# Attention and MoE kernel on one core: Q of six batches loaded four tokens to a partition, and the query order within 64 tokens carried through to the rows of the output stores

## Chip, cores and metric

One core of a Trainium2 chip. The metric is the device time of the kernel in microseconds (us). One run of before took 1761.32 us; it is not used.

## The reference, cut to what matters

```python
# q, k, v: [8, 8, 576, 64] f32; moe_w_in [512, 2048]; moe_w_out [2048, 512]
scores = q @ k.T / sqrt(64); causal, window of 64 keys; softmax; @ v
x = attn.transpose(0, 2, 1, 3).reshape(4608, 512)
h = x @ w_in
out = (h * clip(h + 3, 0, 6) / 6) @ w_out        # [4608, 512] f32
```

## The kernel before

Attention of a batch (576 tokens) runs between the matmuls of the MoE, which works in nine stages T = 0..8 of 512 tokens. A batch b >= 2 is prepared by DMA: load Q, K, V; cast on GpSimd to bf16; two DMA transposes give QT and KT (head dimension on partitions). Its result `opg` goes by three DMA transposes and one on TensorE into `xT`, from which the next MoE stages read. All these DMAs and the output stores are issued by SyncE, in one order.

```python
def load_blocks(t, src, b, kbs, tail=0):          # 128 tokens to 128 partitions: runs of 256 B
    ...
        out.append(nc.sync.dma_start(
            out=t[p0 : p0 + ss, kb, :, :],
            in_=src[b, :, s0 : s0 + ss, :].rearrange("h s d -> s h d"),
        ))

def load_for_dma(b):
    sts, ins = [], []
    for n, src in (("qst", q), ("kst", k), ("vst", v)):
        t = stage.tile([P, KB, H, D], F32, name=n, tag=n)
        ins += load_blocks(t, src, b, range(KB), SR if src is v else 0)
        sts.append(t)
    return tuple(sts), ins

# scores of a pair of heads, then exp on ScalarE and a multiplication by the mask on VectorE
nc.tensor.matmul(st[:, h, o0 : o0 + n], lhsT=bt.KT[...k0 : k0 + P], rhs=bt.QT[...q0 : q0 + n], ...)

# second MoE matmul: 128 tokens to PSUM partitions, copied by ScalarE and stored
nc.scalar.copy(out=osb[:], in_=accs[ts])
...
nc.sync.dma_start(out=out[u0 : u0 + P, :], in_=osb[:])     # 256 KB, rows in order

for T in range(1, NTB):                            # order of issue
    p1, p2 = pieces(nxt); b = T + 2
    if b < B:
        sts, _ = load_for_dma(b)                   # loads of batch T + 2
        ...                                        # casts in the first half of stage T,
        ...                                        # QT, KT transposes late in its second half
    stage_(T, None, p1, p2)                        # attention of batch T + 1, and stores of stage T
```

The softmax here doesn't subtract the row's maximum and nothing guards it: scores larger than these inputs give would overflow.

Of the kernel before, what the change touches and what calls it, by code (L numbers as in the profile page):

```python
# [9 lines left out]
F32 = mybir.dt.float32  # L10
BF16 = mybir.dt.bfloat16
EXP = mybir.ActivationFunctionType.Exp
RELU = mybir.ActivationFunctionType.Relu
MULT = mybir.AluOpType.mult
# [10 lines left out]
def kernel(  # L25
# [9 lines left out]
    nc = tc.nc  # L35
    P = nc.NUM_PARTITIONS
    B, H, S, D = q.shape
# [4 lines left out]
    KB = (S + P - 1) // P  # L42
    SP = KB * P
    R = 4
    SM = P * R
    SR = S - SM
# [4 lines left out]
    QW = P + WINDOW  # L51
# [3 lines left out]
    consts = ctx.enter_context(tc.tile_pool(name="consts", bufs=1))  # L55
    stage = ctx.enter_context(tc.tile_pool(name="stage", bufs=1))
# [31 lines left out]
    def load_blocks(t, src, b, kbs, tail=0):  # L88
        out = []
        for kb in kbs:  # L90
            s0 = kb * P
            ss = min(P, S - s0)
            p0 = tail if ss < P else 0
# [4 lines that stand above are left out]
        return out  # L98

    def load_qk_for_pe(b, heads):  # L100
        qst = stage.tile([P, H, R * D], F32, name="qst", tag="qst")
        kst = stage.tile([P, H, R * D], F32, name="kst", tag="kst")
        rst = stage.tile([P, H, D], F32, name="rst", tag="rst")
        ins = []
        for h0 in range(0, H, heads):
            for dst, src in ((qst, q), (kst, k)):
                ins.append(nc.sync.dma_start(
                    out=dst[:, h0 : h0 + heads, :],
                    in_=src[b, h0 : h0 + heads, 0:SM, :].rearrange("h (p j) d -> p h (j d)", j=R),
                ))  # L110
            if h0 == 0:
                for i, src in enumerate((q, k)):
                    ins.append(nc.sync.dma_start(
                        out=rst[i * SR : (i + 1) * SR, :, :],
                        in_=src[b, :, SM:S, :].rearrange("h s d -> s h d"),
                    ))
        return (qst, kst, rst), ins
# [5 lines left out]

    def load_for_dma(b):
        sts, ins = [], []
        for n, src in (("qst", q), ("kst", k), ("vst", v)):
            t = stage.tile([P, KB, H, D], F32, name=n, tag=n)
            ins += load_blocks(t, src, b, range(KB), SR if src is v else 0)
            sts.append(t)
        return tuple(sts), ins  # L130

    ctx.enter_context(tc.manual_schedule())
    def load_first():
# [28 lines left out]
    def keep_busy(n):  # L162
# [11 lines left out]
        out=mask1[:], in_=mask1[:], pattern=[[1, QW]], compare_op=ISGE,  # L174
# [3 lines left out]
        out=mask1[:], in_=mask1[:], pattern=[[-1, QW]], compare_op=ISGE,  # L178
        fill=0.0, base=WINDOW - 1, channel_multiplier=1,
    )  # L180
    qn_all = consts.tile([P, NG, KB, 2, D], BF16, name="qn")
    kn_all = consts.tile([P, NG, KB, 2, D], BF16, name="kn")
# [3 lines left out]
    for o0, m0, m1 in ((0, 0, QW), (QW, 0, QW), (2 * QW, 0, QW), (3 * QW, 0, P), (3 * QW + P, WINDOW, P)):  # L186
        nc.vector.tensor_scalar(
            out=maskneg[:, o0 : o0 + m1 - m0], in0=mask1[:, m0:m1],
# [25 lines left out]
    fill_v(0)  # L214

    mask = consts.tile([P, 2 * (KB - 1), QW], BF16, name="mask")

    win16 = consts.tile([P, NG, FF], BF16, name="win16")
    wout16 = consts.tile([P, NFC, DM], BF16, name="wout16")
# [14 lines left out]
    vcopy, pcopy, acopy = nc.vector.tensor_copy, nc.gpsimd.tensor_copy, nc.scalar.copy  # L234

    class Batch:
# [10 lines left out]
            copy(out=self.V[SR:P, KB - 1, :, 0:D], in_=vst[SR:P, KB - 1, :, :])  # L247

        def cast_for_dma(self, st, which=(0, 1, 2)):
            for n, s in [((qn_all, st[0]), (kn_all, st[1]))[i] for i in which if i < 2]:  # L250
                for g in range(NG):
                    pcopy(  # L252
                        out=n[:, g, 0 : KB - 1, :, :].rearrange("p k h d -> p k (h d)"),
                        in_=s[:, 0 : KB - 1, 2 * g : 2 * g + 2, :].rearrange("p k h d -> p k (h d)"),
                    )
                pcopy(
                    out=n[:SR, :, KB - 1, :, :].rearrange("p g h d -> p g (h d)"),
                    in_=s[:SR, KB - 1, :, :].rearrange("p (g h) d -> p g (h d)", h=2),
                )
            if 2 in which:  # L260
                self.cast_v(st[2], 0, H, pcopy)
                self.cast_v_end(st[2], pcopy)
# [66 lines left out]
    def scores(bt, g, u, bias=False, bank=None):  # L329


        pT = P_ring[(bt.b * NG + g) % NPT]
        st = ps_st.tile([P, 2, 512], F32, name=f"st{u if bank is None else bank}")
        w = 2 * QW
        if bias:
            for h in range(2):
                nc.tensor.matmul(
                    st[:, h, 0:w], lhsT=ident[:], rhs=maskneg[:, u * w : (u + 1) * w],
                    start=True, stop=False,
                )  # L340
        blocks = (
            ((0, 0, 0, QW), (QW, P, P, QW)),
            ((0, 2 * P, 2 * P, QW), (QW, 3 * P, 3 * P, P), (QW + P, S - P, SM, SR)),
        )[u]
        for o0, k0, q0, n in blocks:
            for h in range(2):
                nc.tensor.matmul(  # L347
                    st[:, h, o0 : o0 + n],
                    lhsT=bt.KT[h * D : (h + 1) * D, g, k0 : k0 + P],
                    rhs=bt.QT[h * D : (h + 1) * D, g, q0 : q0 + n],  # L350
                    start=not bias, stop=not bias or o0 == blocks[-1][0],
                )

        def exps():
            nc.scalar.activation(  # L355
                out=pT[:, :, 2 * u : 2 * u + 2, 0:QW],
                in_=st[:, :, 0:w].rearrange("p h (k w) -> p h k w", k=2),
                func=EXP, scale=scale,
            )

        return exps

    def masked(bt, g):
        pT = P_ring[(bt.b * NG + g) % NPT]
        nc.vector.tensor_tensor(  # L365
            out=pT[:, :, :, 0:QW], in0=pT[:, :, :, 0:QW],
            in1=mask[:].rearrange("p (h k) w -> p h k w", h=2), op=MULT,
        )

    opgs = {}  # L370
# [82 lines left out]
    oa = o_acc()  # L453


    gTs = {}
    held = []

# [37 lines left out]
    def s2(T, order):  # L496

        gT, accs = gTs[T], {}
        for ts, u in order:
            if u == 0:  # L500
                accs[ts] = next(oa)
            for fc in range(4 * u, 4 * u + 4):
                nc.tensor.matmul(  # L503
                    accs[ts], lhsT=gT[:, fc, ts * P : (ts + 1) * P], rhs=wout16[:, fc, :],
                    start=(fc == 0), stop=(fc == NFC - 1),
                )
            if u == 3:
                osb = osbp.tile([P, DM], F32, name="osb")
                nc.scalar.copy(out=osb[:], in_=accs[ts])  # L509
                u0 = T * TB + ts * P  # L510
                if T:
                    nc.sync.dma_start(out=out[u0 : u0 + P, :], in_=osb[:])
                else:
                    held.append((u0, osb))
            yield
# [26 lines left out]
    def S_(bt, g, u):  # L542
        later[bt.b, "s", g, u] = scores(bt, g, u)
# [21 lines left out]
    def SS(bt, g):  # L565
        S_(bt, g, 0)
        S_(bt, g, 1)
        do(bt, "s", g, 0)
        do(bt, "s", g, 1)
        masked(bt, g)  # L570
# [6 lines left out]
    bt, st = Batch(0), stage0  # L577
# [12 lines left out]
    def S0_(g, u):  # L590
        later[0, "s", g, u] = scores(bt, g, u, bias=True, bank=(u if g > 1 else g))
# [50 lines left out]
    st1, ins = load_qk_for_pe(1, 4)  # L642
    for x in ins:
# [5 lines left out]
        out=mask[:], in_=mask1[:].unsqueeze(1).to_broadcast([P, 2 * (KB - 1), QW])  # L649
    )  # L650
    for h in range(2):
        nc.vector.tensor_copy(
            out=mask[:, (KB - 1) * (h + 1) - 1, P:QW], in_=mask1[:, WINDOW : 2 * WINDOW],
        )
    bt, st = Batch(1), st1
# [14 lines left out]
    for g in range(NG):  # L670
        bt.cast_v(vst1, 2 * g, 2 * g + 2, pcopy)
    st2, _ = load_for_dma(2)

    m = s2(0, BY_QUARTER)
    S_(bt, 0, 0)
    RR(bt, oa_tr)
# [6 lines left out]
    for g in range(1, NG):  # L683
        if g > 1:
            run(m, 2)
        S_(bt, g, 0)
        if g + 1 < NG:
            T_(bt, g + 1)
        if g == 1:
            run(m, 2)  # L690
        S_(bt, g, 1)
        if g + 1 < NG:
            do(bt, "q", g + 1)
        masked(bt, g - 1)
        do(bt, "s", g, 0)
        if g + 1 < NG:
            do(bt, "k", g + 1)
        do(bt, "s", g, 1)
    run(m, 2)
    masked(bt, 3)  # L700
    run(m, 2)
    for g in range(NG):
# [27 lines left out]
    def pieces(bt):  # L730
# [14 lines left out]
        }  # L745
        return p1, p2

    bt2 = Batch(2)
    bt2.cast_for_dma(st2, (0, 1))
    for u0, osb in held:  # L750
# [4 lines left out]
    for T in range(1, NTB):  # L755
        p1, p2 = pieces(nxt)
        b = T + 2
        nxt = None
        if b < B:
            sts, _ = load_for_dma(b)  # L760
# [36 lines left out]
```

## Time and profile before

| | before |
|---|---|
| time, median | 321.14 us (319.27, 321.14 and 321.56 in the three normal runs) |
| span of the profiled run | 317.6 us |
| TensorE busy | 300.8 us, 95% |
| TensorE waits for DMA after 60 us | 3.4 us |

One stage in the table of stretches (us; busy us and instructions of PE, PEld, DVE, ACT, POOL; granted clock, mean share of time that packets took on the 16 DMA engines, GB/s):

```profile
162.00:194.00 32.00, 31.79 (x234) 15.81 (x238) 19.72 (x36) 19.17 (x29) 9.71 (x13) 1.00 1.04 203
```

The list of waits of TensorE from 60 us on (what waited, for whom: us in total, times, longest):

```profile
PE st L347 <- DMA KT<-kn: 2.4, 2, 2.0
PE st L466 <- DMA xT<-opg: 1.0, 1, 1.0
```

These 3.4 us are what earlier DMAs could save.

Last, two pieces of the chain that ended last in before: the landing of an xT transpose that stage 3 waits for, and the last copy of the kernel (the span ends 317.6 - 314.5 = 3.1 us after it):

```profile
128.11 2.62 DMA xT<-opg
...
313.93 0.59 ACT osb L509
```

And the group of the wide score matmuls of before (count | busy us, mean ns | idle before them):

```profile
L347 PE MATMUL st<-QT,KT 64*128 64x192 bf16 x192 | 14.9, 247 | 4.2 <-DMA KT<-kn 2.4 <-ACT KT L316 1.5 <-ACT pT L355 0.2
```

### The profile page before, as it was taken

The page shows a single profiled execution, that of the slowest core. Times are in us where ns is not written, and L with a number is a line of the kernel's source. Part 1 is how long each engine was busy: PE and PEld are TensorE (multiplying, and loading weights), DVE is VectorE, ACT ScalarE, POOL GpSimd, SP SyncE. Part 2 cuts the span into 40 slices and gives each one's busy share as a digit, 9 for nine tenths or more (in the row PEclk, how much of TensorE's full clock was granted, in tenths as well). Part 3 has the DMA queues.
Part 4 walks back from the last instruction along what each step waited for, and adds up shares of the span by engine and source line. Part 5 has one row for each costly group of instructions (what it writes and reads, how often), then busy time and mean ns, then how long its engine had stood idle before and what let it go on. Part 6 is the DMA issues. An engine that isn't in the chain of part 4 may idle for free.

```text
span 317.6 us, 5604 instructions
## 1 busy us (share of the span) xinstructions
PE 300.8 (95%) x2131; PEld 149.5 (47%) x2167; DVE 173.9 (55%) x331; ACT 177.9 (56%) x265; POOL 85.7 (27%) x131
## 2 busy tenths in 40 slices
PE   8989799999999799899999999999999999999995
PEld 3454345544554355344544554445444544444442
DVE  4658643476636665277527853785378438406700
ACT  2748753387637771487258725872587347417711
POOL 5741805363045143305610650065000000000000
PEclk9999999999999999999999999999999999999999
DMA  8999999999799999999999998999800630010011
GB/s 211 237 173 253 238 199 205 204 184 248 158 208 209 270 215 205 191 254 204 195 257 210 207 184 208 211 201 185 204 34 2 122 75 0 28 73 33 0 68 66
DMA packets 150843, 52.64 MB, mean 166 GB/s; under 512 B 138272, under 2 KB 146464, under 8 KB 150816
## 3 DMA queue, kind: packets, MB, share of 16 engines
q1 hardware_dynamic: 146000, 46.77, 72.7%
q0 software_dynamic: 4544, 5.24, 9.5%
q8 instruction: 17, 0.28, 0.4%
q10 hardware_dynamic: 272, 0.26, 0.2%
q14 instruction: 10, 0.08, 0.1%
HBM read 36.70 MB, written 9.44 MB: 145 GB/s over the span
## 4 chain that ended last, share of the span: by engine, by line
PE 63%; DMA 21%; SPq 8%; POOL 3%; issue 2%; DVE 1%; ACT 1%; POOLq 0%
PE o L503 15%; PE acc L503 14%; PE hT L466 14%; PE acc L466 5%; PE o L466 5%; SPq L94 5%; DMA vst<-in_v_dram 4%; DMA kst<-in_k_dram 4%; DMA KT<-kn 4%; DMA qst<-in_q_dram 3%; PE st L466 3%; PE st L347 3%; DMA wout<-in_moe_w_out_dram 3%; DMA win<-in_moe_w_in_dram 3%; PE hT L377 1%
## 5 line engine op out<-in xcount | busy, mean ns | idle before, releaser
L466 PEld LDWEIGHTS <-win 128*128 128x128 bf16 x576 | 55.3, 98 | 67.2 <-issue 2.3
L503 PEld LDWEIGHTS <-gT 128*128 128x128 bf16 x576 | 52.9, 98 | 57.5 <-issue 0.6
L503 PE MATMUL o<-wout,gT 128*128 128x512 bf16 x274 | 67.5, 379 | 1.5 <-DMA wout<-in_moe_w_out_dram 0.7
L503 PE MATMUL acc<-wout,gT 128*128 128x512 bf16 x278 | 67.1, 379 | 0.7 <-issue 0.3
L466 PE MATMUL hT<-xT,win 128*128 128x512 bf16 x266 | 65.7, 379 | 0.3
L355 ACT ACTIVATE pT<-st 128x768 bf16<-128x768 f32 x64 | 48.9, 813 | 10.8 <-PE st L347 10.7
L473 ACT ACTIVATE t<-hT,half 128x512 bf16<-128x512 f32 x68 | 46.7, 690 | 9.6 <-PE hT L466 9.2
L474 DVE SCALAR_TENSOR_TENSOR gT<-t,hT 128x512 bf16<-128x512 bf16 x68 | 46.4, 685 | 9.4 <-ACT t L473 9.1
L474 DVE SCALAR_TENSOR_TENSOR gT<-t,st 128x512 bf16<-128x512 bf16 (+1 forms) x26 | 19.7, 768 | 52.9 <-ACT t L473 52.9
L365 DVE TENSOR_TENSOR pT<-pT,mask 128x1536 bf16<-128x1536 bf16 x28 | 28.1, 1004 | 23.0 <-ACT pT L355 23.0
L509 ACT COPY osb<-o 128x512 f32<-128x512 f32 x18 | 10.6, 586 | 46.2 <-PE o L503 46.2
L252 POOL CAST qn<-qst 128x512 bf16<-128x512 f32 x24 | 16.1, 712 | 74.1 <-DMA qst<-in_q_dram 59.7
L509 ACT COPY osb<-acc 128x512 f32<-128x512 f32 x18 | 10.6, 587 | 35.7 <-PE acc L503 33.7
L466 PE MATMUL st<-xT,win 128*128 128x512 bf16 x117 | 28.2, 379 | 1.7 <-DMA xT<-opg 1.0
L397 DVE TENSOR_TENSOR opg<-hT,rec 128x320 bf16<-128x320 f32 x56 | 27.5, 492 | 1.9
L466 PE MATMUL acc<-xT,win 128*128 128x512 bf16 x91 | 23.6, 379 | 0.1
L466 PE MATMUL o<-xT,win 128*128 128x512 bf16 x90 | 23.5, 379 | 0.1
L473 ACT ACTIVATE t<-st,half 128x512 bf16<-128x512 f32 (+1 forms) x26 | 19.4, 752 | 7.2 <-PE st L466 7.1
L377 PEld LDWEIGHTS <-pT 128*128 128x128 bf16 x256 | 17.8, 97 | 9.1 <-issue 1.4
L347 PE MATMUL st<-QT,KT 64*128 64x192 bf16 (+2 forms) x320 | 17.9, 229 | 4.2 <-DMA KT<-kn 2.4
L394 DVE RECIPROCAL rec<-hT 128x5 f32<-128x5 f32 x56 | 10.5, 188 | 20.0 <-PE hT L386 19.9
L243 POOL CAST V<-vst 128x512 bf16<-128x512 f32 (+1 forms) x14 | 16.4, 1168 | 17.4 <-DMA vst<-in_v_dram 17.0
(76 smaller groups left out, 269.2 us busy)
## 6 DMA issues: line engine op xcount, KB each, us to landing
out_dram<-osb SPq DMA_DIRECT2D x32, 256.0 KB, 2.4
qst<-in_q_dram SPq DMA_DIRECT2D x28, 256.0 KB, 4.7
kst<-in_k_dram SPq DMA_DIRECT2D x27, 256.0 KB, 5.4
vst<-in_v_dram SPq DMA_DIRECT2D x24, 256.0 KB, 5.1
vst<-in_v_dram SPq DMA_DIRECT2D x24, 128.0 KB, 4.1
win<-in_moe_w_in_dram POOLq DMA_DIRECT2D x4, 512.0 KB, 7.6
wout<-in_moe_w_out_dram POOLq DMA_DIRECT2D x4, 512.0 KB, 8.8
qst<-in_q_dram SPq DMA_DIRECT2D x2, 512.0 KB, 6.1
```

The lines of the kernel that those rows point to most:

```text
L243: copy(out=self.V[:, 0 : KB - 1, h0:h1, 0:D], in_=vst[:, 0 : KB - 1, h0:h1, :])
L252: pcopy(out=n[:, g, 0 : KB - 1, :, :].rearrange("p k h d -> p k (h d)"), in_=s[:, 0 : KB - 1, 2 * g : 2 * g + 2, :].rearrange("p k h d -> ...
L347: nc.tensor.matmul(st[:, h, o0 : o0 + n], lhsT=bt.KT[h * D : (h + 1) * D, g, k0 : k0 + P], rhs=bt.QT[h * D : (h + 1) * D, g, q0 : q0 + n], ...
L355: nc.scalar.activation(out=pT[:, :, 2 * u : 2 * u + 2, 0:QW], in_=st[:, :, 0:w].rearrange("p h (k w) -> p h k w", k=2), func=EXP, scale=scale,
L365: nc.vector.tensor_tensor(out=pT[:, :, :, 0:QW], in0=pT[:, :, :, 0:QW], in1=mask[:].rearrange("p (h k) w -> p h k w", h=2), op=MULT,)
L377: nc.tensor.matmul(ob, lhsT=pT[:, h, qb, 0:P], rhs=V[:, qb, 2 * g + h, :], start=True, stop=(qb == 0),)
L397: nc.vector.tensor_tensor(out=opgs[bt.b, g][:, :, h, :], in0=ov[:, :, 0:D], in1=rec[:].unsqueeze(2).to_broadcast([P, KB, D]), op=MULT,)
L466: nc.tensor.matmul(hT, lhsT=win16[:, g, fc * P : (fc + 1) * P], rhs=xT[:, g, t0 : t0 + TB], start=(g == 0), stop=(g == NG - 1),)
L473: nc.scalar.activation(out=t1[:], in_=hT, func=RELU, bias=half[:], scale=1.0 / 6.0)
L474: nc.vector.scalar_tensor_tensor(out=out, in0=t1[:], scalar=1.0, in1=hT, op0=MIN, op1=MULT,)
L503: nc.tensor.matmul(accs[ts], lhsT=gT[:, fc, ts * P : (ts + 1) * P], rhs=wout16[:, fc, :], start=(fc == 0), stop=(fc == NFC - 1),)
L509: nc.scalar.copy(out=osb[:], in_=accs[ts])
```

## The change

The intent: Q arrives in runs of 1 KB (four tokens of a head to a partition), a quarter of the packets and three issues instead of five. The price is an order: after the transpose the queries of a batch stand as (j, a, s), where token = 64 a + 4 s + j. The score matmuls read them as (a, j, s), so queries are permuted only within 64 tokens. A second, permuted mask matches. The order then lasts through softmax, V, both MoE matmuls, and is undone by the DRAM side of the stores, in two pieces of 64 rows.

```diff
     def load_for_dma(b):
         sts, ins = [], []
-        for n, src in (("qst", q), ("kst", k), ("vst", v)):
+        qst = stage.tile([P, H, R * D], F32, name="qst", tag="qst")
+        rst = stage.tile([P, H, D], F32, name="rst", tag="rst")
+        for h0 in range(0, H, 4):
+            ins.append(nc.sync.dma_start(
+                out=qst[:, h0 : h0 + 4, :],
+                in_=q[b, h0 : h0 + 4, 0:SM, :].rearrange("h (p j) d -> p h (j d)", j=R),
+            ))
+        ins.append(nc.sync.dma_start(
+            out=rst[0:SR, :, :], in_=q[b, :, SM:S, :].rearrange("h s d -> s h d"),
+        ))
+        for n, src in (("kst", k), ("vst", v)):
 ... (the cast of Q on GpSimd follows the new layout: the same sizes)
+        if bt.b > 1:
+            for i in range(2):
+                for h in range(2):
+                    kb = 2 * u + i
+                    n = min(3, (SM - kb * P) // SR)
+                    nc.tensor.matmul(
+                        st[:, h, i * QW : i * QW + n * SR].rearrange("p (a j s) -> p a j s", j=R, s=SR // R),
+                        lhsT=bt.KT[h * D : (h + 1) * D, g, kb * P : (kb + 1) * P],
+                        rhs=bt.QT[h * D : (h + 1) * D, g, 0:SM].rearrange(
+                            "d (j a s) -> d a j s", j=R, s=SR // R
+                        )[:, 2 * kb : 2 * kb + n, :, :],
+                        start=True, stop=True,
+                    )
 ... (the last 64 queries: read with a step of 4)
-            in1=mask[:].rearrange("p (h k) w -> p h k w", h=2), op=MULT,
+            in1=(mask if bt.b < 2 else maskj)[:].rearrange("p (h k) w -> p h k w", h=2), op=MULT,
+    def store(u0, osb):
+        n = max(0, min(P, 2 * S - u0))
+        if n:
+            nc.sync.dma_start(out=out[u0 : u0 + n, :], in_=osb[0:n, :])
+        for c in range(n, P, SR):
+            nc.sync.dma_start(
+                out=out[u0 + c : u0 + c + SR, :].rearrange("(s j) f -> j s f", j=R), in_=osb[c : c + SR, :],
+            )
-                    nc.sync.dma_start(out=out[u0 : u0 + P, :], in_=osb[:])
+                    store(u0, osb)
 ... (one copy on VectorE makes maskj from mask)
```

More of the change, by code (lines that the diff above doesn't have):

```diff
@@ L129, in load_for_dma @@
             sts.append(t)
-        return tuple(sts), ins
+        return ((qst, rst), *sts), ins
     ctx.enter_context(tc.manual_schedule())
@@ L216 @@
     mask = consts.tile([P, 2 * (KB - 1), QW], BF16, name="mask")
+    maskj = consts.tile([P, 2 * (KB - 1), QW], BF16, name="maskj")
     win16 = consts.tile([P, NG, FF], BF16, name="win16")
@@ L249, in cast_for_dma @@
         def cast_for_dma(self, st, which=(0, 1, 2)):
-            for n, s in [((qn_all, st[0]), (kn_all, st[1]))[i] for i in which if i < 2]:
+            for i in which:
+                if i > 1:
+                    continue
+                n = (qn_all, kn_all)[i]
                 for g in range(NG):
-                    pcopy(
-                        out=n[:, g, 0 : KB - 1, :, :].rearrange("p k h d -> p k (h d)"),
-                        in_=s[:, 0 : KB - 1, 2 * g : 2 * g + 2, :].rearrange("p k h d -> p k (h d)"),
-                    )
+                    if i:
+                        pcopy(
+                            out=n[:, g, 0 : KB - 1, :, :].rearrange("p k h d -> p k (h d)"),
+                            in_=st[1][:, 0 : KB - 1, 2 * g : 2 * g + 2, :].rearrange("p k h d -> p k (h d)"),
+                        )
+                    else:
+                        pcopy(
+                            out=n[:, g, 0 : KB - 1, :, :],
+                            in_=st[0][0][:, 2 * g : 2 * g + 2, :].rearrange("p h (j d) -> p j h d", j=R),
+                        )
+                rest = st[1][:SR, KB - 1, :, :] if i else st[0][1][:SR, :, :]
                 pcopy(
                     out=n[:SR, :, KB - 1, :, :].rearrange("p g h d -> p g (h d)"),
-                    in_=s[:SR, KB - 1, :, :].rearrange("p (g h) d -> p g (h d)", h=2),
+                    in_=rest.rearrange("p (g h) d -> p g (h d)", h=2),
                 )
@@ L340, in scores @@
                 )
+        if bt.b > 1:
+            QJ = P // R
+            for i in range(2):
[9 more added lines that the diff above has]
+                        start=True, stop=True,
+                    )
+            if u:
+                for h in range(2):
+                    nc.tensor.matmul(
+                        st[:, h, QW + P : 2 * QW].rearrange("p (j s) -> p j s", j=R),
+                        lhsT=bt.KT[h * D : (h + 1) * D, g, S - P : S],
+                        rhs=bt.QT[h * D : (h + 1) * D, g, SM:S].rearrange("d (s j) -> d j s", j=R),
+                        start=True, stop=True,
+                    )
         blocks = (
@@ L344, in scores @@
         )[u]
-        for o0, k0, q0, n in blocks:
+        for o0, k0, q0, n in blocks if bt.b < 2 else ():
             for h in range(2):
@@ L453 @@
     oa = o_acc()
+    def store(u0, osb):
[5 more added lines that the diff above has]
+                out=out[u0 + c : u0 + c + SR, :].rearrange("(s j) f -> j s f", j=R), in_=osb[c : c + SR, :],
+            )
     gTs = {}
@@ L746, in pieces @@
         return p1, p2
+    nc.vector.tensor_copy(
+        out=maskj[:].rearrange("p n (a j s) -> p (n a) j s", j=R, s=SR // R),
+        in_=mask[:].rearrange("p n (a s j) -> p (n a) j s", j=R, s=SR // R),
+    )
     bt2 = Batch(2)
```

## The prediction

> **What bounds it now.** TensorE is busy 300.8 of 317.6 us (busy table). From 131 us on it never pauses: the table of stretches gives 31.8 of each 32 us, matmuls following each other every 0.216 us. Before that the chain of waits runs through loads, casts and DMA transposes, but TensorE has other work meanwhile: after 60 us the list of waits shows only 2.4 us for KT (0.43 at 76.6, 1.97 at 106.7) and 1.04 us for xT at 130.8. Those 3.4 us are nearly all that faster loads can win; the first 60 us are not touched.
>
> **What the change removes.** Q of a batch is 4096 runs of 256 B plus the tail; it becomes 1024 runs of 1 KB. By the DMA records a 256 B packet takes 22.5 ns, a 1 KB packet on the same queue 56.6 ns. My estimate per engine and batch: 256 x 22.5 = 5.8 us becomes 64 x 56.6 = 3.6 us, so 2 us per batch, and about 4 us by batch 3. That should end the 1.97 and 0.43 us waits, and probably the 1.04.
>
> **What it adds.**
> - Stores. Of 32 stores from the SyncE queue, 27 (outputs from row 1152 on) become pairs of 128 KB, one more issue of 0.5 us each. [...] The new DRAM side is "j s f" with j = 4 outermost: k would be 4. No transfer of this trace can show it. Then a 256 KB store is 32 packets of 2 KB on each of four engines, at 85 ns 2.7 us, where it was 8 packets, 0.7 us, on each of 16. In a 32 us stage those four engines take on 4 x 2 = 8 us and lose 2 us of Q. By my estimate (864 load and 440 transpose packets at 16 to 19 ns, 32 store packets) they were busy 26 us of 32; they would be full, 32 of 32. The transposes of xT behind a store would land up to 2.7 us later; their slack at stage starts is some 2 to 4 us.
> - The end. The last store is on the path for certain: +2 to +2.5 us with four engines (+0.5 if it still uses 16).
> - VectorE: one permuting copy of 128x1536 bf16, estimate 0.6 to 1.7 us (the plain copy took 607 ns), near 60 us, where VectorE idles over 4 us: free.
> - TensorE: the same number and width of score matmuls; the query side is read in runs of 16 elements, the last 64 with a step of 4. At most 1 to 2 us.
>
> **Sum.** -3.4 (waits) + 2.2 (end) + about 1 (some stage starts waiting for xT or QT behind stores) = about 0. From fast runs of 319.3 to 321.1 I predict 320.0 us, range 315.5 to 326. Chances: faster 0.04, same 0.86, slower 0.10.
>
> **What would show it.** The completion packets of 4 B on the queue (3536 now) tell k. TensorE waits for KT near 77 and 107 us gone; store landing of 2.4 us (median) rising to 3 or more; a longer gap from the last copy to the end; score matmuls still 247 ns for 192 columns.
>
> **What would make it wrong.** Stores keep 16 engines: 317. Four full engines hold back loads and transposes in every stage: over 326. Strided query reads slow TensorE, which has no slack.

Here k is the number of DMA engines that a store is spread over. k = 4 was my assumption, and the two store terms (+2.2 at the end, about +1 at stage starts) rest on it. The sum came to -3.4 + 2.2 + about 1, about 0, hence 320.0 us.

## More of the kernel before

From the page of before: the busy line, the granted clock of TensorE in 40 slices of the span (in tenths of full speed; 9 is 90% or more), and the count of DMA packets.

```profile
PE 300.8 (95%) x2131; PEld 149.5 (47%) x2167; DVE 173.9 (55%) x331; ACT 177.9 (56%) x265; POOL 85.7 (27%) x131
PEclk9999999999999999999999999999999999999999
DMA packets 150843, 52.64 MB, mean 166 GB/s; under 512 B 138272, under 2 KB 146464, under 8 KB 150816
```

TensorE hardly pauses and its clock is full in every slice (mean granted clock 1.000).

Next, one cycle of the DMA queue that SyncE issues, from the QT transpose of one batch to that of the next (start us, us that the issues took, what, count):

```profile
130.07 2.64 SPq L266 DMA_TRANSPOSE QT<-qn  x1
132.81 3.49 SPq L266 DMA_TRANSPOSE KT<-kn  x1
136.39 0.54 SPq L512 DMA_DIRECT2D out_dram<-osb  x1
136.98 4.24 SPq L94 DMA_DIRECT2D qst<-in_q_dram  x5
141.26 5.83 SPq L94 DMA_DIRECT2D kst<-in_k_dram  x5
147.18 6.82 SPq L94 DMA_DIRECT2D vst<-in_v_dram  x5
154.11 0.57 SPq L512 DMA_DIRECT2D out_dram<-osb  x1
154.77 2.58 SPq L418 DMA_TRANSPOSE xT<-opg  x2
157.45 0.53 SPq L512 DMA_DIRECT2D out_dram<-osb  x1
158.08 1.24 SPq L418 DMA_TRANSPOSE xT<-opg  x1
159.45 0.50 SPq L512 DMA_DIRECT2D out_dram<-osb  x1
160.05 2.60 SPq L266 DMA_TRANSPOSE QT<-qn  x1
```

The cycle takes 160.05 - 130.07 = 30.0 us, and TensorE's stage takes 32: the queue keeps up, with only 2 us to spare (the next two cycles take 31.9 and 32.0 us, TensorE's pace).

## The result, and the profile after

Ratios here and below are the mean time of one kernel's fast runs over that of the other's of the same rounds, so not quite the ratio of the medians quoted beside them. Executions over 1.5% slower than the fastest of the same kernel are left out of the means.

After: median 345.3 us (344.11 to 347.65, 4 runs), before 321.14 us (three normal runs). Ratio 1.0778, 95% interval 1.0687 to 1.0868: slower by 24 us, outside the range of 315.5 to 326. The profiled span went from 317.6 to 342.6 us, 25.0 us more.

The same lines of the page after:

```profile
PE 309.7 (90%) x2131; PEld 151.2 (44%) x2167; DVE 175.7 (51%) x332; ACT 177.8 (52%) x265; POOL 85.7 (25%) x131
PEclk9999999999999998999879998999989999999998
DMA packets 132003, 52.64 MB, mean 154 GB/s; under 512 B 113288, under 2 KB 127624, under 8 KB 131976
```

The packet count answers the open question of the prediction. It fell by 150843 - 132003 = 18840. Q accounts for 6 x (4096 - 1024) = 18432. The other 408 are packets of 4 B (3536 on the queue in before, 3128 in after), which I count as completion packets, one from every engine that works on a DMA. In the raw records of before each of the 201 DMAs raises its semaphore 16 times. In after 162 DMAs do the same, and the 54 store halves raise it five times, once early and four times later (the one issued at 138.40 us: at 0.95 us, then at 5.84 to 7.16 us). 12 load DMAs fewer at 16 each are 192, and 27 stores at 16 (432) that became 54 at k each leave 432 - 54 k = 216, so k = 4. That the four stand for four engines is my reading; the landings below fit it.

TensorE now loses full clock in four groups of slices (0.50 granted from 168.8 to 175.5 us, for one; and also in the last slice, where it has almost nothing left to do). Its waits from 60 us on:

```profile
PE st L518 <- DMA xT<-opg: 14.8, 5, 4.6
```

The waits for KT are gone, as predicted; those for xT grew from 1.0 to 14.8 us. The cycle of the SyncE queue, from QT to QT of the same two batches:

```profile
129.59 4.33 SPq L287 DMA_TRANSPOSE QT<-qn  x1
134.01 3.71 SPq L287 DMA_TRANSPOSE KT<-kn  x1
137.81 1.12 SPq L504 DMA_DIRECT2D out_dram<-osb  x2
138.99 1.82 SPq L129 DMA_DIRECT2D qst<-in_q_dram  x2
140.86 0.73 SPq L133 DMA_DIRECT2D rst<-in_q_dram  x1
141.64 9.95 SPq L94 DMA_DIRECT2D kst<-in_k_dram  x5
151.69 5.98 SPq L94 DMA_DIRECT2D vst<-in_v_dram  x5
157.76 1.27 SPq L504 DMA_DIRECT2D out_dram<-osb  x2
159.15 4.32 SPq L461 DMA_TRANSPOSE xT<-opg  x2
163.56 1.13 SPq L504 DMA_DIRECT2D out_dram<-osb  x2
164.78 2.94 SPq L461 DMA_TRANSPOSE xT<-opg  x1
167.81 1.12 SPq L504 DMA_DIRECT2D out_dram<-osb  x2
169.05 5.02 SPq L287 DMA_TRANSPOSE QT<-qn  x1
```

The cycle is now 169.05 - 129.59 = 39.5 us, and the next two are 38.6 and 37.9 (QT at 207.63 and 245.54). Everything behind a store takes longer to issue: QT and KT 8.0 us instead of 6.1, the three xT transposes 7.3 instead of 3.8. Q itself issues in 2.6 us instead of 4.2, but K behind it needs 9.95 instead of 5.83. And the third xT transpose lands late. Pieces of the chain after (start us, us), from its issue to the end:

```profile
164.78 5.35 DMA xT<-opg
170.18 2.72 PE st L518 x6
172.90 3.10 PE hT L518 x8
...
335.77 0.59 ACT osb L561
```

The transpose takes 5.35 us from issue to landing, where before it took 2.62. TensorE has waited 4.62 us for it, and then its 14 matmuls take 2.72 + 3.10 = 5.82 us, where the same two pieces of before (at 130.77 us) took 1.46 + 1.73 = 3.19: the granted clock was 0.54 over the 5.82 us, where it was 1.00 in before. At the four stage starts with such a wait these 14 take 20.43 us in all instead of 12.76. The end of the span comes 342.6 - 336.4 = 6.2 us after the last copy, before it was 3.1.

An account of the 25.0 us: waits for DMA +11.4 (14.8 against 3.4), matmuls at lowered clock +7.7, the end +3.1; 2.8 stay unassigned. The score matmuls, for which the prediction allowed 1 to 2 us (a guess), cost nothing at 192 columns (247 before); only the 64-column ones read with a step of 4 went from 190 to 214 ns:

```profile
L368 PE MATMUL st<-QT,KT 64*128 64x192 bf16 x144 | 10.3, 246 | 0.2 <-ACT pT L398 0.2
L378 PE MATMUL st<-QT,KT 64*128 64x64 bf16 x48 | 5.2, 214 | 0.0
```

### The profile page after: what moved, and what is told of

The parts are those of the page before. It is cut to its first block, busy times and chain, and to the rows that moved or that the text cites. A ratio compares the mean times of both kernels' runs of the same rounds, so it can differ in the third digit from the quotient of the medians.

```text
span 342.6 us, 5613 instructions
## 1 busy us (share of the span) xinstructions
PE 309.7 (90%) x2131; PEld 151.2 (44%) x2167; DVE 175.7 (51%) x332; ACT 177.8 (52%) x265; POOL 85.7 (25%) x131
## 2 busy tenths in 40 slices
DMA packets 132003, 52.64 MB, mean 154 GB/s; under 512 B 113288, under 2 KB 127624, under 8 KB 131976
## 3 DMA queue, kind: packets, MB, share of 16 engines
q0 software_dynamic: 4544, 5.24, 8.4%
## 4 chain that ended last, share of the span: by engine, by line
PE 70%; DMA 16%; SPq 5%; DVE 2%; ACT 2%; issue 1%; POOL 1%; POOLq 0%
PE hT L518 16%; PE o L555 16%; PE acc L555 13%; DMA xT<-opg 6%; PE st L518 6%; PE acc L518 6%; PE o L518 6%; PE st L368 3%; DMA wout<-in_moe_w_out_dram 3%; DMA kst<-in_k_dram 3%; DMA win<-in_moe_w_in_dram 2%; PE hT L420 2%; DMA vst<-in_v_dram 1%; DMA qst<-in_q_dram 1%; PE hT L425 1%
## 5 line engine op out<-in xcount | busy, mean ns | idle before, releaser
L518 PEld LDWEIGHTS <-win 128*128 128x128 bf16 x576 | 57.2, 101 | 88.2 <-issue 28.3
L518 PE MATMUL hT<-xT,win 128*128 128x512 bf16 x266 | 69.9, 398 | 0.3
L518 PE MATMUL st<-xT,win 128*128 128x512 bf16 x117 | 32.7, 415 | 15.6 <-DMA xT<-opg 14.8
L408 DVE TENSOR_TENSOR pT<-pT,maskj 128x1536 bf16<-128x1536 bf16 x24 | 25.2, 1050 | 19.3 <-ACT pT L398 19.3
L267 POOL CAST kn<-kst 128x512 bf16<-128x512 f32 x24 | 14.8, 657 | 25.6 <-DMA kst<-in_k_dram 25.6
```

The lines of the kernel that those rows point to most:

```text
L267: pcopy(out=n[:, g, 0 : KB - 1, :, :].rearrange("p k h d -> p k (h d)"), in_=st[1][:, 0 : KB - 1, 2 * g : 2 * g + 2, :].rearrange("p k h d ...
L408: nc.vector.tensor_tensor(out=pT[:, :, :, 0:QW], in0=pT[:, :, :, 0:QW], in1=(mask if bt.b < 2 else maskj)[:].rearrange("p (h k) w -> p h k ...
L518: nc.tensor.matmul(hT, lhsT=win16[:, g, fc * P : (fc + 1) * P], rhs=xT[:, g, t0 : t0 + TB], start=(g == 0), stop=(g == NG - 1),)
```

## The experiments

Theory A: a store on 4 of 16 DMA engines gives these four more work than a stage has time for, and as every load and transpose works on all sixteen (it raises its semaphore 16 times in the traces), the whole queue slows to their pace. Rivals: the Q half or the permuted scores (B), the number of issues (C), the lowered clock as a cost of its own (D), the order in one queue (E). Fourteen runs were made in four groups, each group beside runs of before on the same chip. A kernel marked "wrong" gives rows in another order, with the same amount of work. Engines in the table are k, by the packet counts.

| run | what | median us | ratio to before (95%) |
|---|---|---|---|
| after | the change | 345.3 | 1.078 (1.069 to 1.087) |
| e1_store_only | only the store half | 354.25 | 1.103 (1.096 to 1.110) |
| e2_q_only | only the Q half | 318.31 | 0.993 (0.988 to 0.997) |
| e3_pairs16 | pairs of stores, 16 engines | 318.79 | 0.993 (0.988 to 0.999) |
| e5_store_k8 | 8 engines | 320.4 | 0.996 (0.992 to 1.000) |
| e10_k4_single | 4 engines, one store instead of two | 347.12 | 1.082 (1.077 to 1.087) |
| e12_store_k2 | 2 engines | 385.94 (one run, state unknown) | |
| e14_k4_late | 4 engines, only after the last load | 321.14 | 1.000 (0.996 to 1.005) |
| e6_busy | matmuls without use in the waits | 346.39 | 1.077 (1.073 to 1.082) |
| e8_store_act | stores from the ScalarE queue | 351.84 | 1.094 (1.087 to 1.102) |
| e9_store_pool | stores from GpSimd | 334.8 | none |
| e4_psum_order | natural order made in PSUM | 324.86 | 1.013 (1.008 to 1.018) |
| e7_rhs_order | natural order made in the query read | 339.02 | 1.057 (1.052 to 1.063) |
| e11_exp_order, e13_exp_again | natural order made in the exponential | 322.01, 319.6 | 0.989 (two of six runs count as fast), 0.996 (0.992 to 1.000) |

### The two halves alone: e1_store_only, e2_q_only

```diff
  # e1_store_only: the kernel before, rows wrong on purpose
-                    nc.sync.dma_start(out=out[u0 : u0 + P, :], in_=osb[:])
+                    store(u0, osb)          # store() of the change
```

> The kernel before with only its stores changed: rows from 1152 on leave in pairs of 128 KB whose DRAM side has the dimension of 4 outermost (row order wrong on purpose). Theory A (a store on 4 of 16 DMA engines overloads these four and delays the xT transposes behind it): 341 to 352 us, completion packets 3320, TensorE waits of 3 to 5 us for xT at four stage starts with a lowered clock after them. Rival B (the 1 KB Q loads, the permuted score reads or the VectorE copy cost the time): 319 to 324 us.

```diff
  # e2_q_only: the kernel after, rows wrong on purpose
     def store(u0, osb):
-        ... (pairs)
+        nc.sync.dma_start(out=out[u0 : u0 + P, :], in_=osb[:])
```

> The kernel after with the plain 256 KB stores of before (row order wrong on purpose): 1 KB Q loads, permuted scores and the second mask stay. What the Q half is worth alone. My count: the TensorE waits for KT and xT after 60 us (3.4 us in before) go, nothing is added: 316 to 319 us, 0.986 to 0.995 of before. If permuted score reads cost TensorE time: at or above before.

e1 took 354.25 us and e2 318.31. The waits of TensorE in e1 from 60 us on:

```profile
PE st L475 <- DMA xT<-opg: 20.7, 8, 8.0
PE st L347 <- DMA KT<-kn: 2.6, 2, 2.0
```

So the stores alone cost more than the whole change: 354.25 lies a little above the range given for theory A, and B falls. The Q half alone is worth 2.2 us, 0.7%, and clears both waits to 0.6 us. The two do not add. With the stores in place the Q half saves about 8 us (the ratio falls from 1.103 to 1.078), nearly four times what it saves alone, since the queue has become the bottleneck. In the profiles the 2.6 us of waits for KT go, and three cycles of the queue from QT to QT take 115.95 us instead of 120.77, 1.6 less each; the prediction had costed 2 us for a batch.

### How many engines, how many issues: e3_pairs16, e5_store_k8, e12_store_k2, e10_k4_single

```diff
  # e3_pairs16 (rows wrong on purpose)
-                out=out[u0 + c : u0 + c + SR, :].rearrange("(s j) f -> j s f", j=R), in_=osb[c : c + SR, :],
+                out=out[u0 + c : u0 + c + SR, :], in_=osb[c : c + SR, :],
  # e5_store_k8: j=2 * R;  e12_store_k2: j=R // 2;  (rows wrong on purpose)
  # e10_k4_single (rows wrong on purpose)
+            nc.sync.dma_start(
+                out=out[u0 : u0 + P, :].rearrange("(s j) f -> j s f", j=R), in_=osb[:],
+            )
```

> The kernel after with its pairs of 128 KB stores kept, but plain rows (64 partitions to 64 consecutive rows, order wrong on purpose). Theory A: 16 engines again, completion packets 3776, 316 to 320 us. Rival C (twice the number of store issues on the SyncE queue costs the time): over 335 us. Rival B: about 345 us.

> The kernel after with 8 instead of 4 as the outermost dimension of the stores (row order wrong on purpose). Theory A: 8 engines, completion packets 3344, each of them busy about 29 of 32 us per stage: 318 to 327 us, xT landing under 4 us. If the permuted row order in HBM itself costs, not the number of engines: about 345 us.

> The kernel after with 2 outermost in the stores (row order wrong on purpose). Theory A in numbers: an engine has about 22 us of loads and transposes a stage; with k = 4 it gets 11 us of stores on top (33), with k = 2 it gets 22 (44). After's measured period of 38 to 39 us should grow by 44/33 to about 51, over four to five periods: 390 to 415 us, completion packets 3020. If only the latency of a store in the queue counts: under 375 us.

> The kernel after with each pair of 128 KB stores made one of 256 KB with 4 outermost (row order wrong on purpose): same four engines and bytes, half the issues and half the places in the window of 8 outstanding DMAs. Capacity of four engines (theory A): 341 to 348 us, as after. If the number of issues or the window counts: 330 us or less.

First, that k was what the expectations say. The packet count of e3's page:

```profile
DMA packets 132651, 52.64 MB, mean 166 GB/s; under 512 B 113936, under 2 KB 128272, under 8 KB 132624
```

And that of e5's page:

```profile
DMA packets 132219, 52.64 MB, mean 165 GB/s; under 512 B 113504, under 2 KB 127840, under 8 KB 132192
```

They are 648 = 54 x 12 and 216 = 54 x 4 above after's 132003: k = 16 and 8. (e12 has 108 fewer, k = 2.) The times follow k. A stage stores 512 rows of 2 KB; a packet of that size takes 85 ns in the DMA records of before (median), and the second and third columns are estimates from these, with the rows shared evenly by k engines.

| engines k | 2 KB packets per engine and stage | at 85 ns | QT to QT | time |
|---|---|---|---|---|
| 16 (e3) | 32 | 2.7 us | 31.6 us | 318.79 us |
| 8 (e5) | 64 | 5.4 us | 32.7 us | 320.4 us |
| 4 (after) | 128 | 10.9 us | 38.6 us | 345.3 us |
| 2 (e12) | 256 | 21.8 us | 47.3 us | 385.94 us |

Down to k = 8 the cycle stays near the 32 us that TensorE needs for a stage. From 8 to 4 the engines get 5.4 us more and the cycle grows by 5.9; from 4 to 2 they get 10.9 more and it grows by 8.7. This fits engines that run out of time in a stage; that they do so is argued from it, not shown. e12's 385.94 us (one run) misses both expectations: a little under the 390 to 415 that I had worked out (a cycle of 51 us; its 22 us of loads and transposes are 1048 packets at 18 ns and 64 at 46, the medians of 256 B and 1 KB in after), well over the 375 of the rival. Nor is it the permuted row order itself that costs, as e5 permutes rows too.

The traces show the few engines more directly. A load's semaphore is raised 16 times, and I take each raise for the landing of one engine's part. For the first Q load behind two stores these raises came so (us after its issue):

| engines k of the stores | Q load issued at | first raises | the other raises |
|---|---|---|---|
| 16 (e3) | 136.09 | 16 at 3.7 to 4.1 | none |
| 8 (e5) | 135.67 | 8 at 3.6 to 3.7 | 8 at 4.0 to 5.5 |
| 4 (after) | 138.99 | 12 at 3.5 to 4.3 | 4 at 7.2 to 8.2 |
| 2 (e12) | 144.08 | 14 at 3.9 to 4.3 | 2 at 9.4 to 10.3 |

With k = 4 and 2, as many raises lag clearly as the packet count gives the stores engines. By this reading, what needs all sixteen is held back: the 16 raises of the third xT transpose of the cycle come together, 5.2 to 5.4 us after its issue (164.78) in after, 2.6 to 2.8 us (158.08) in before. And after issues its third K load at 147.30 us, when this Q load has just landed in full (138.99 + 8.21 = 147.20). The lag lies behind the stores: the last part of a V load lands on average 5.4 us after its issue both in before and in after. TensorE's waits for xT in e12:

```profile
PE st L518 <- DMA xT<-opg: 42.9, 9, 6.9
```

The number of issues is out as a cause: e3 issues as many stores as after and is faster than before; e10 issues half as many on the same four engines and is as slow as after (347.12 us, ratio 1.082 against 1.078). The window of 8 that its expectation names is seen in the trace of after: SyncE's DMAs go round eight semaphores, each of the 195 from the ninth on with that of the eighth before it, whose raises were complete by then. With half the places in it taken the time is the same.

### Only where the engines are shared: e14_k4_late

```diff
-        n = max(0, min(P, 2 * S - u0))
+        n = P if u0 < 6 * TB else 0
```

> The kernel after with store pairs on 4 engines only in stages 6 to 8 (12 of 36 stores), plain stores before (order of those rows wrong on purpose). Theory A (they cost only where loads and transposes need the same engines, plus the last store): e2_q_only's 318.3 plus 3 us for the end, 319 to 323 us, no TensorE waits for xT. If four-engine stores cost by themselves (12 of 27, so about 12 of after's 27 us over e2): 328 us and more.

Result 321.14 us, ratio 1.000, beside the 0.993 of e2: about 2.5 us, the size of the longer end (there the span ends 319.3 - 313.1 = 6.2 us after the last copy, in e2 3.4 us). From 60 us on TensorE waits for no DMA. So four-engine stores after the last load cost no more than that end; in after, where others stand beside loads and transposes too, the ratio is 1.078.

### The lowered clock: e6_busy

```diff
+    def fill_gap(n):
+        for b in range(2):
+            gap = h_bank()
+            for _ in range(n // 2):
+                nc.tensor.matmul(gap[:], lhsT=win16[:, 0, 0:P], rhs=xT[:, 0, 0:TB], start=True, stop=True)
 ...
         for i in range(16):                        # second half of a stage
             run(m, 1)
             for f in pieces2.get(i, ()):
                 f()
+        if 1 < T < 6:
+            fill_gap(16)
```

> The kernel after with 16 matmuls without use (3.5 us) put where TensorE waits for xT at the starts of stages 3 to 6. Theory D (the wait also lowers the granted clock, and the first 14 to 16 matmuls after it then cost about 2.2 us more, four times): DMA sets when a stage starts, clock 1.00 there, 335 to 340 us. Rival (the clock falls for another reason, or the wait is set by TensorE's own chain): 345 us or more, up to 359.

It took 346.39 us: theory D falls, although its mechanism works. TensorE of e6 around the start of stage 4 (start us, us):

```profile
163.57 3.62 PE L768 MATMUL hT<-xT,win 128*128 128x512 bf16 x16
167.02 0.59 PE L518 MATMUL st<-xT,win 128*128 128x512 bf16 x2
169.63 1.46 PE L518 MATMUL st<-xT,win 128*128 128x512 bf16 x6 [2.01 <-DMA xT<-opg]
170.92 1.89 PE L518 MATMUL hT<-xT,win 128*128 128x512 bf16 x8
```

The eight matmuls take 1.89 us instead of 3.30 in the same view of after, as in before at full clock (1.89 us at 164.09 us, granted clock 1.00), so the clock is kept here. But the starts after the waits come at 169.63, 208.42 and 247.63 us, in after at 170.18, 208.82 and 246.94: DMA sets them. What TensorE gains within a stage it waits at the next one: the four fillings (4 x 3.45 us) and the waits for xT and KT (6.5 + 2.9) make 23.2 us in e6, the waits and slow matmuls of after 14.8 + 7.7 = 22.5. So the 7.7 us that the account above puts down to the clock are not a second cause: waits and slow matmuls together are the difference between DMA's cycle and TensorE's stage.

How long a wait went before slow matmuls can be read from the traces. After the gaps of 3.00, 4.62, 3.36 and 3.33 us in after the granted clock is 0.50 (131.2 to 134.5, 168.8 to 175.5, 209.7 to 213.0 and 247.3 to 250.6 us); after the 1.97 us of before it is 1.00 (106.7 to 112.0 us). In e6 a gap of 2.66 us, at 208.42 us, was already enough (after six more matmuls at full speed the next eight took 3.58 us), and gaps of 2.01 and 1.79 us were not.

### Other queues for the same stores: e8_store_act, e9_store_pool

```diff
-            nc.sync.dma_start(                     # in store(), the pairs only
+            nc.scalar.dma_start(                   # e8;  e9: nc.gpsimd.dma_start(
```

> The kernel after with its store pairs issued from the ScalarE queue: the same 4 engines and packets, correct result. If the loss is that the loads and transposes wait in one in-order queue behind stores (theory E): 318 to 327 us. If it is that four engines have more work than a stage has time (theory A as I costed it, 32 of 32 us): 335 us and more. In between both count.

> The kernel after with its store pairs issued from GpSimd (software descriptors); correct result. [...] If the loss is the load on four fixed engines: 316 to 323 us. If k = 4 in itself is slow or GpSimd's order (stores before the casts of the next batch) costs: 330 us and more.

e8 took 351.84 us. With the stores out of the SyncE queue its cycle was still 39.4 and 41.2 us from QT to QT, which speaks against E, as does the landing of its first Q load there (issued at 139.70 us): 12 raises at 3.8 to 4.3 us, four at 6.4 to 7.1, as if the stores stood in the same queue. But it is not clean: at two stage ends the store waited on ScalarE until the QT transpose had landed (at 139.56 and 179.55 us), and ScalarE stood still for 8.2 and 6.8 us. e9 took 334.8 us, between the two expectations, with runs from 328.82 to 339.53 of which only the fastest counts as fast, so it has no ratio. TensorE there waits for KT, not for xT (14.3 us in its profile, taken in a run counted slow). Moving the stores to GpSimd cuts the loss and brings another wait; what it says of the engines stays open. (Of the expectation of e9, "four fixed engines" and "software descriptors" are my assumptions; of the latter the page of before shows that GpSimd's 12 DMAs, 5.24 MB, went through a queue of the kind software_dynamic.)

### The Q half in a correct kernel: e4_psum_order, e7_rhs_order, e11_exp_order, e13_exp_again

The stores need no permuted rows if the natural order is restored earlier. Three places were tried, all with the Q loads of the change, plain 256 KB stores and the old mask; all three are correct.

```diff
  # e4_psum_order: the matmul writes PSUM with a step of 4
-  st[...].rearrange("p (a j s) -> p a j s", ...)
+  st[...].rearrange("p (a s j) -> p a j s", ...)
  # e7_rhs_order: the matmul reads the queries with a step of 128 elements
-  rhs=bt.QT[...].rearrange("d (j a s) -> d a j s", ...)
+  rhs=bt.QT[...].rearrange("d (j a s) -> d a s j", ...)
  # e11_exp_order and e13_exp_again (the same kernel): the exponential reads PSUM with a step of 16
-  nc.scalar.activation(out=pT[:, :, ...], in_=st[...], func=EXP, scale=scale)
+  for h in range(2):
+      nc.scalar.activation(
+          out=o[:, h, :, :].rearrange("p k (a s j) -> p k a s j", j=R, s=SR // R),
+          in_=i[:, h, :, :].rearrange("p k (a j s) -> p k a s j", j=R, s=SR // R), func=EXP, scale=scale)
```

> A correct kernel with the 1 KB Q loads and plain stores: the score matmuls read the queries in runs of 16 and write their PSUM columns with a step of 4, so that the query order is natural from there on; no second mask. If a stepped PSUM write costs no TensorE time, 192-column score matmuls stay at 246 ns and the time equals that of e2_q_only, 316 to 319 us. If it costs, they go to 300 ns and more and the time to 320 and above.

> As e4_psum_order, but the natural order is made on the read side: queries are read with a step of 128 elements in SBUF and written to PSUM in a row. The 64-column matmuls read with a step of 4 took 214 ns in the kernel after against 190 to 192 unstepped, so a stepped read seems to cost about 0.35 ns a column: 192 columns at 300 to 320 ns, the time 1 to 8 us above e4_psum_order. If no difference, the 214 ns had another cause.

> A correct kernel with the 1 KB Q loads and plain stores: matmuls as in after, but the exponential on ScalarE reads PSUM with a step of 16 and writes the natural order; for that it is cut in two per step (384 columns, about 0.58 us each by the line through 0.69 us for 512 and 1.11 for 1024, against 0.81). TensorE costs nothing, ScalarE 0.36 us a step on an engine with 44% slack: 316 to 320 us, 0.988 to 1.0 of before, and then better than before. If stepped PSUM reads are slow on ScalarE too: its busy time rises by over 20 us and the time goes to 322 and more.

> The kernel of e11_exp_order again. If its fast group is the kernel's own time: most runs 316 to 318 us, ratio 0.985 to 0.993. If it truly alternates between two states: again some runs near 322. If 322 is its time: ratio 1.00 to 1.01.

The 192-column score matmuls of e4:

```profile
L367 PE MATMUL st<-QT,KT 64*128 64x192 bf16 x144 | 15.9, 353 | 0.0
```

The same group of e7:

```profile
L367 PE MATMUL st<-QT,KT 64*128 64x192 bf16 x144 | 27.3, 494 | 0.0
```

Against 246 ns in after, a stepped write costs 107 ns and a stepped read 248 ns. TensorE has no slack (busy 31.8 of a stage's 32 us in before), so e4 (324.86 us) and e7 (339.02 us) lose more than the 2.2 us that Q is worth. I had hoped that the write would be free and put the read at 300 to 320 ns; both were too low.

ScalarE reads PSUM in steps without a loss that shows: its busy time in e13 is 180.4 us, in before 177.9. The exponentials of e13 that read stepped, and those of batches 0 and 1 that do not:

```profile
L400 ACT ACTIVATE pT<-st 128x384 bf16<-128x384 f32 x96 | 39.3, 512 | 2.4 <-PE st L367 2.4
L406 ACT ACTIVATE pT<-st 128x768 bf16<-128x768 f32 x16 | 12.7, 816 | 7.1 <-PE st L389 7.0
```

Half the columns take 512 ns where I had estimated 0.58 us for an unstepped read; no unstepped exponential of this width was run. In the first try (e11) two normal runs took 316 to 317 us and three 322; the ratio of 0.989 rests on the two, since the others count as slow. The sixth run took 1761.11 us and is not used: in its trace 12 matmuls of 512 columns take 15.87 us, 1.32 us each against 0.216 in before, six times slower, while the granted clock reads 1.000; what slowed it stays open. In the second (e13) all six lie between 317.93 and 320.98, ratio 0.996, interval 0.992 to 1.000. So the best correct version found is level with before or up to 1% faster; a gain is not shown.

## Why the prediction was wrong

- Right: what bounds the kernel; that only 3.4 us were to be won from waits; k = 4, which was assumed; about 2 us of DMA time per batch for Q (1.6 us a cycle from e1 to after); the score matmuls at 246 ns; the VectorE copy in a gap (it took 0.95 us). The Q half alone gave 2.2 us of those 3.4.
- Right in kind, small in size: the end. It grew by 3.1 us, predicted 2 to 2.5.
- The step that failed is the term "about 1 (some stage starts waiting for xT or QT behind stores)". It measured 22.5 us in the profile (14.8 of waits for xT, and 7.7 of slow matmuls that belong to them). The reasoning before it had the mechanism: four engines "would be full, 32 of 32", each store 2.7 us on them. From there it went on as if the only effect were that a transpose lands up to 2.7 us later, and set that against a slack of 2 to 4 us.
- Why that step misled: the estimate left no room at all, and it was too low. Its 26 us before the change took 16 to 19 ns for a packet of 256 B (18 is the median in the records of before), while the saving of Q was reckoned with the mean of 22.5. With that mean the 864 + 440 packets and the stores make 29.3 + 2.7 = 32 us already before the change. And the table of stretches that the prediction cites gave a DMA share of 1.22, 1.04 and 1.02 from 131 to 226 us (mean of 16 engines; over 1, so packet records overlap). The measured cycle was 38 to 39.5 us. A cycle that is longer than TensorE's 32 us uses up any slack in the first stage and then costs its excess in every one: here 7.4, 6.6 and 6.1 us from one late start to the next (130.8, 170.2, 208.8 and 246.9 us), after 3.0 us at the first, in sum 23.1 us, near the 22.5 above (of which 1.7 fall after the last of these starts). The case was named under what would make the prediction wrong, but given 0.10.
- What the term should have been can be seen from the experiments: the cycle for k = 4 less 32 us, times the stages that still load. The 38.6 us could not have been read from the trace of before; that 32 of 32 is no margin could have been.
- Not foreseen and of no consequence: the lowered clock (e6).
- Open: the trace does not name the engine of a packet. In the landings four raises of 16 lag behind the stores (7.2 to 8.2 us against 3.5 to 4.3), which I read as four engines that the rest waits for; that these four are full all through a stage is not shown. Their stage work is 33 us by the packet times I used and 43 us by the mean times in the trace of after (24 ns for 256 B, 55 ns for 1 KB, 111 ns for 2 KB, for 1048, 64 and 128 packets); the cycle lies between. How much of it is full engines and how much the order of one queue is not settled, as e8 was not clean.

## What to carry to other kernels

Look at the outermost dimension of the DRAM side of a store before changing its shape: here a permutation with 4 outermost moved a store from 16 completion packets to 4, by my reading from 16 engines to 4, and the time from 321 to 345 us, while one with 8 outermost left it at 320.4 us (ratio 0.996). Where a queue is near the pace of the compute (here cycles of 30 to 32 us beside a stage of 32), cost a change for the busiest engine, and treat a sum that just fills the stage as a slowdown, not as a draw. If a layout has to be undone, undo it on an engine that has slack and reads it at little cost, here ScalarE's read of PSUM (busy 180.4 us against 177.9 in before), rather than on the bottleneck engine or in the DMA.
